# Retention attention and a Mish MLP on one core: half products of four feature blocks placed around the last outputs of the head, an earlier Mish table, factors in one operation

## The chip, the cores and the metric

The kernel runs on one core of a Trainium2 chip. The metric is the device time of one execution in microseconds; lower is better. A core has a matrix engine (TensorE, PE in the profile; its weight loads are PEld), a vector engine (VectorE, DVE), a scalar engine with function tables (ScalarE, ACT), a general engine (GpSimd, POOL) and a synchronisation engine (SyncE, SP). Each works through its own list of instructions in order and waits on semaphores. Products land in PSUM, which has eight banks of 512 float32 values in each of 128 partitions; everything else works out of SBUF. In this kernel POOL issues the loads and SP most stores.

## The reference, cut to what matters

```
# q, k, v: (8 batches, 8 heads, 576 positions, 64)
scores = q @ k.T / 8
gamma  = 1 - 2 ** (-5 - head)
Dmat   = where(i >= j, gamma ** (i - j), 0)
ret    = (scores * Dmat) @ v
x      = ret.transpose(0, 2, 1, 3).reshape(4608, 512)
h      = x @ w_in                      # 512 x 2048
g      = h * tanh(log(1 + exp(h)))     # Mish
out    = g @ w_out                     # 2048 x 512
```

## The kernel before

The 4608 tokens are cut into chunks of 128 (576 = 4 x 128 + 64, the last 64 of two batches make one chunk), and four chunks make a tile of 512 tokens. There are nine tiles. For each tile the attention gives xT (the features by the tokens, in four slices of 128 features), the first dense product with w_in gives 16 feature blocks f = 0 to 15 of 128, Mish on ScalarE turns each into gT, and the second dense product with w_out gives the output. The order of all instructions on each engine is written out by hand; from about 17 us on the dense products run on TensorE without a break, and the attention of later tiles is placed between them.

The change lies in the head, that is what runs before the dense products of the first tile. The first tile is the first 128 positions of batches 0 to 3, and no state is needed for it:

- Constants (L125 to L165). POOL's iota writes dist. VectorE makes late (L152), dist (L153), dmask for eight heads (L156), ident (L158) and pos (L160), then ex, one column of five per head (L661). ScalarE takes exponentials: dmask (L659), then gq (L662) and gv (L663).
- `f_transpose(t, g, i, parts)` turns k (i = 1) or q (i = 0) of the two batches of group g on TensorE (L203) into one or two PSUM banks, and each bank is evicted by the engine that parts names (L208).
- `f_scores(0, g)` makes the scores of two batches (L222), and VectorE multiplies them by dmask into sm (L226): four operations per group.
- `f_v(0, b, copy)` casts v of batch b into vb (L236).
- `f_out(0, b, copy)` is the product of vb and sm (L254), evicted into xT's columns of batch b (L258).
- `turn_back(g)` (L272) turns keys back for a later stage, and `keep_warm` (L170, L173) issues products of zeros.
- ScalarE's Mish table is loaded by a Mish of one column, warm (L674), between `f_v(0, 0)` and `f_v(0, 1)`.
- `g1_half(f)` (L565) multiplies only the first 256 columns of xT, the batches 0 and 1, for a feature block; `g1(0, f, 2, begun)` adds the other half and then runs Mish (L590). `g1_pair(2)` takes f = 2 and 3 whole, in two banks of two pools, with a Mish each at L577.
- `product` (L553) can be halved: two products of 256 columns (L558) take the place of one of 512. The count `halved` says how many of the next ones are.

PSUM is given out by pools: ps_sc has two tiles of two banks ("sc"), ps_st one bank ("st"), ps_h two of one bank ("hp"), ps_o one ("ops"). The framework sets the semaphores: an instruction waits for those before it in the program that touch the same data.

Of the kernel before, what the change touches and what calls it, by code (L numbers as in the profile page):

```python
# [9 lines left out]
F32 = mybir.dt.float32  # L10
BF16 = mybir.dt.bfloat16
AX = mybir.ActivationFunctionType
OP = mybir.AluOpType
# [3 lines left out]
def kernel(  # L17
# [18 lines left out]
    nc = tc.nc  # L36
    B, H, S, D = q.shape
    assert (B, H, S, D) == (8, 8, 576, 64)
    P = 128
# [4 lines left out]
    KC = d_model // P  # L44
    NCH = 4
# [17 lines left out]
    consts = ctx.enter_context(tc.tile_pool(name="consts", bufs=1))  # L63
# [7 lines left out]
    op = ctx.enter_context(tc.tile_pool(name="op", bufs=4))  # L71
    PS = bass.MemoryType.PSUM
    ps_sc = ctx.enter_context(tc.tile_pool(name="ps_sc", bufs=2, space=PS))
    ps_st = ctx.enter_context(tc.tile_pool(name="ps_st", bufs=1, space=PS))
    ps_h = ctx.enter_context(tc.tile_pool(name="ps_h", bufs=2, space=PS))
    ps_o = ctx.enter_context(tc.tile_pool(name="ps_o", bufs=1, space=PS))
# [4 lines left out]
    w_in_t = wpool.tile([P, KC, d_ff], BF16)  # L81
# [15 lines left out]
    gts = {0: gp.tile([P, nF, NCH * P], BF16, name="gT")}  # L97
# [29 lines left out]
    lnd = consts.tile([P, 1], F32)  # L127
# [5 lines left out]
    pos = consts.tile([P, 5], F32)  # L133
    for c in range(5):
        nc.vector.memset(pos[:, c:c + 1], float(P * c))
    nc.vector.memset(pos[64:P, 4:5], 512.0 - 64.0)
    minus_p = consts.tile([P, 1], F32)
    late = consts.tile([P, P], F32)
    for i in (1, 0):
        for b in (2, 3):  # L140
# [6 lines left out]
    for f0 in (512, 768):  # L147
        load_w_in(f0, 256)
    mask = consts.tile([P, 64], F32)
    lg = [math.log(1.0 - 2.0 ** (-5.0 - h)) for h in range(H)]  # L150
    nc.vector.tensor_copy(minus_p, dist[:, 0:1])
    nc.vector.tensor_scalar(late, dist, 0.0, 1.0e6, op0=OP.is_lt, op1=OP.mult)  # L152
    nc.vector.tensor_tensor(dist, dist, late, op=OP.max)  # L153
    dmask = consts.tile([P, H, P], F32)
    for h in range(H):
        nc.vector.tensor_scalar(dmask[:, h, :], dist, lg[h], None, op0=OP.mult)  # L156
    ex = consts.tile([P, 5, H], F32)
    nc.vector.tensor_scalar(ident, dist, 0.0, None, op0=OP.is_equal)  # L158

    nc.vector.tensor_scalar(pos, pos, minus_p, None, op0=OP.subtract)  # L160
    gqk = consts.tile([P, 5, 2, H], F32)
    nc.vector.memset(gqk, 1.0)
    gq = gqk[:, :, 0, :]
    gv = consts.tile([P, 5, H], F32)
    warm = consts.tile([P, 25], F32)  # L165

    def keep_warm(n, pool=ps_o, name="ops", long=0):
        idle = pool.tile([P, 512], F32, name=name)
# [6 lines left out]
    xts = {}  # L175
# [12 lines left out]
    def f_transpose(t, g, i, parts):  # L188

        name = ("qb", "kb")[i]  # L190
        out_t = tr.tile([P, 2, NP, P], BF16, name="qkT", bufs=6).rearrange("p i n t -> p (i n) t")
        n = 8 // len(parts)
        moves = []
        for j, (pool, tname, copy) in enumerate(parts):
            tp = pool.tile([P, 2, 8, P] if tname == "sc" else [P, 8, P], BF16, name=tname)
            tp = (tp[:, 0] if tname == "sc" else tp)[:, 0:n]
            for r in range(n):
                if t == 1:
                    mix = fst[1][name, "mix", g][:, n * j + r]
                    nc.tensor.transpose(tp[:, r, :], mix.rearrange("p x d -> p (x d)"), ident)  # L200
                else:
                    for x in range(2):
                        nc.tensor.transpose(tp[ds(64 * x, 64), r, :],  # L203
                                            fst[0][name][:, 2 * g + x, ts(n * j + r, D)], ident)
            moves.append((copy, out_t.rearrange("p h (g r) -> p h g r", r=8)[:, :, :, ds(n * j, n)],
                          tp.rearrange("p r (g h) -> p h g r", h=H)))
        for copy, to, src in moves:
            copy(to, src)  # L208
        fst[t][name, g] = out_t
# [21 lines left out]
    def f_v(t, b, copy):  # L231
        vb = first.tile([P, H, D], BF16, name="vb", bufs=4)
        copies = copy if isinstance(copy, tuple) else (copy,)
        n = H // len(copies)
        for j, copy in enumerate(copies):
            copy(vb[:, ds(n * j, n), :], v0[4 * t + b][:, ds(n * j, n), :])  # L236
        fst[t]["vb"][b] = vb
        if t == 1:
            v0s[4 + b] = vb

    def f_out(t, b, copy):
        if b == 0:
            xts[t] = xp.tile([P, KC, NCH * P], BF16, name="xT")
        vb = fst[t]["vb"][b]
        if t == 0:
            pool, name = ((ps_h, "hp"), (ps_h, "hp"), (ps_st, "st"), (ps_o, "ops"))[b]
            ot = pool.tile([P, NP, P], F32, name=name)
        else:
            if b % 2 == 0:
                fst[1]["out"] = ps_sc.tile([P, 2, NP, P], F32, name="sc")  # L250
            ot = fst[1]["out"][:, b % 2]
        for p in range(NP):
            for e in range(2):
                nc.tensor.matmul(ot[ds(64 * e, 64), p, :], lhsT=vb[:, 2 * p + e, :],  # L254
                                 rhs=fst[t]["sm", b][:, 2 * p + e, :],
                                 start=(p == 0), stop=True, skip_group_check=True)
        if t == 0:
            copy(xts[t][:, :, ts(b, P)], ot)  # L258
        elif b % 2:
            copy(xts[1].rearrange("p h (b i) -> p b h i", i=P)[:, ds(b - 1, 2)], fst[1]["out"])  # L260
# [285 lines left out]
    halved = [0]  # L546
# [4 lines left out]
    def product(to, w, x, first, last):  # L551
        if first or last or not halved[0]:
            newest[0] = nc.tensor.matmul(to, lhsT=w, rhs=x, start=first, stop=last)  # L553
            return
        halved[0] -= 1
        n = x.shape[-1] // 2
        for j in range(2):
            nc.tensor.matmul(to[:, ts(j, n)], lhsT=w, rhs=x[:, ts(j, n)], start=False, stop=False,  # L558
                             skip_group_check=True)

    def g1_half(f):
        hp = ps_h.tile([P, NCH * P], F32, name="hp")
        n = NCH * P // 2
        for c in range(KC):
            nc.tensor.matmul(hp[:, 0:n], lhsT=w_in_t[:, c, ts(f, P)], rhs=xts[0][:, c, 0:n],  # L565
                             start=(c == 0), stop=(c == KC - 1))
        return hp

    def g1_pair(f0):
        banks = [ps_o.tile([P, NCH * P], F32, name="ops"), ps_h.tile([P, NCH * P], F32, name="hp")]  # L570
        for cs in ((0, 1), (2, 3)):
            for f in range(2):
                for c in cs:
                    halved[0] = int(c == 1)
                    product(banks[f], w_in_t[:, c, ts(f0 + f, P)], xts[0][:, c, :], c == 0, c == KC - 1)
        for f in range(2):
            nc.scalar.activation(gts[0][:, f0 + f, :], banks[f], AX.Mish)  # L577

    def g1(t, f, parts=1, begun=None):
        if t not in gts:  # L580
            gts[t] = gp.tile([P, nF, NCH * P], BF16, name="gT")
        if begun is not None:
            hp = begun
        else:
            hp = ps_h.tile([P, NCH * P], F32, name="hp")
        n = NCH * P // parts
        for j in range(0 if begun is None else 1, parts):
            for c in range(KC):
                product(hp[:, ts(j, n)], w_in_t[:, c, ts(f, P)], xts[t][:, c, ts(j, n)], c == 0, c == KC - 1)
        done = nc.scalar.activation(gts[t][:, f, :], hp, AX.Mish)  # L590
        if (t, f) in gated:
            load(gated[t, f], done)
            queued[0] += 1
# [62 lines left out]
    dve, act, pool = nc.vector.tensor_copy, nc.scalar.copy, nc.gpsimd.tensor_copy  # L656


    nc.scalar.activation(dmask, dmask, AX.Exp, bias=lnd[:, 0:1])  # L659
    for h in range(H):  # L660
        nc.vector.tensor_scalar(ex[:, :, h], pos, lg[h], None, op0=OP.mult)  # L661
    nc.scalar.activation(gq, ex, AX.Exp)  # L662
    nc.scalar.activation(gv, ex, AX.Exp, scale=-1.0)  # L663
    for b in range(2):
        dve(fst[0]["qb"][:, b, :], q0[:, b, :])
    keep_warm(4, long=4)
    f_transpose(0, 0, 1, [(ps_h, "hp", act), (ps_h, "hp", dve)])
    f_transpose(0, 0, 0, [(ps_st, "st", act), (ps_o, "ops", dve)])
    keep_warm(1, ps_sc, "sc")
    f_transpose(0, 1, 1, [(ps_h, "hp", act), (ps_h, "hp", act)])  # L670
    f_scores(0, 0)
    f_transpose(0, 1, 0, [(ps_st, "st", act), (ps_o, "ops", act)])
    f_v(0, 0, pool)
    nc.scalar.activation(warm[:, 0:1], lnd, AX.Mish)  # L674
    f_v(0, 1, act)
    load_w_in(1024, 512)
    keep_warm(1, ps_h, "hp", long=1)
# [7 lines left out]
    load_w_in(1536, 512)  # L685
    f_v(0, 3, (dve, dve))
    f_v(0, 2, (act, pool))
    f_out(0, 3, dve)
    f_out(0, 2, act)
    begun = [g1_half(0), g1_half(1)]  # L690
    for i, b in ((1, 0), (1, 1), (0, 0), (0, 1)):
        load_first_qk(1, i, b)
    for i in range(2):
# [20 lines left out]

    for f in range(2):
        g1(0, f, 2, begun[f])
    g1_pair(2)
    for f in range(4, nF):
        halved[0] = (f > 6) + (f > 8)
        g1(0, f)  # L720
    for i in range(2):
        f_mix(0, i)
# [1 line left out]
    for i in range(nF):  # L724
        for step in steps.get(i, "").split():
            n = int(step[1])
# [171 lines left out]
```

## Time and profile before

| | us |
|---|---|
| median of 3 runs | 296.61 |
| lowest and highest | 296.42, 296.66 |
| the profiled execution | 297.28 |
| its span, first to last instruction | 295.6 |
| TensorE busy in the span | 286.1 |
| VectorE, ScalarE, POOL busy | 140.0, 128.1, 124.9 |
| HBM read and written, MB | 37.75, 9.44 |

The profile is one execution seen by the hardware. A row of the timeline has the start in us from the span's start, the busy time, the engine, the line of the kernel, the operation, what it writes and reads, the shape and the count; in brackets stands how long the engine was idle before it and what ended that. In a row that merges several instructions the busy time is their union. Products on TensorE are pipelined: one of 128x512 is shown with 0.38 us, but the next can start earlier, so lengths of stages are better read off the starts. A row of waits names the waiting engine and line, what it waited for, the total in us, the count and the longest. Landings are times from the issue of a transfer to its last byte.

### The profile page before, as it was taken

To read this page: it belongs to the slowest core of one execution; us is meant where nothing else is said; L and a number is where in the kernel's file an instruction comes from. 1 tells how busy PE (TensorE), PEld (TensorE's weight loads), DVE (VectorE), ACT (ScalarE), POOL (GpSimd) and SP (SyncE) were. 2 spreads that over 40 slices of the span, in tenths; PEclk is the share of its full clock that TensorE was granted. 3 is DMA by queue.
4 is the path that set the end of the run, shared out by engine and by line. 5 is a ranking of instruction groups with operands and counts; after the bars stand their busy time and mean duration, and the time that the engine had idled before them with its cause. 6 is when DMAs were issued, how large, how long until landed. Compare 5 with 4: busy or idle time off the path is not lost.

```text
span 295.6 us, 7898 instructions
## 1 busy us (share of the span) xinstructions
PE 286.1 (97%) x3447; PEld 159.7 (54%) x3486; DVE 140.0 (47%) x252; ACT 128.1 (43%) x210; POOL 124.9 (42%) x163
## 2 busy tenths in 40 slices
PE   7899999999999999999999999999999999999995
PEld 4666887556567454447645454545454544444443
DVE  5861549399954829454655454535453221000011
ACT  3856226776545534443443434343435333333200
POOL 8944678880167195855483636392020000000000
PEclk9999999999999999999999999999999999999999
DMA  7999999982498889799476837374222111011121
GB/s 154 234 204 204 205 328 337 336 237 85 109 270 190 168 229 254 232 145 330 116 204 164 260 90 237 108 229 115 68 71 71 38 38 65 9 35 49 59 71 71
DMA packets 44067, 47.45 MB, mean 161 GB/s; under 512 B 25984, under 2 KB 33152, under 8 KB 44032
## 3 DMA queue, kind: packets, MB, share of 16 engines
q0 software_dynamic: 15120, 31.20, 41.6%
q1 hardware_dynamic: 28768, 15.54, 20.7%
q8 instruction: 27, 0.44, 0.6%
q10 hardware_dynamic: 144, 0.20, 0.2%
q14 instruction: 8, 0.07, 0.1%
HBM read 37.75 MB, written 9.44 MB: 160 GB/s over the span
## 4 chain that ended last, share of the span: by engine, by line
PE 93%; DMA 2%; issue 1%; ACT 1%; POOL 1%; DVE 0%; POOLq 0%
PE hp L553 41%; PE ops L553 30%; PE hp L558 6%; PE ops L558 4%; DMA gT<-in_q_dram 2%; PE sc L373 1%; PE sc L428 1%; PE hp L504 1%; PE hp L487 1%; PE hp L634 1%; PE st L558 1%; POOL gT L107 1%; PE st L428 1%; PE sc L351 1%; PE sc L200 1%
## 5 line engine op out<-in xcount | busy, mean ns | idle before, releaser
L553 PE MATMUL hp<-xT,w_in_t 128*128 128x512 bf16 (+1 forms) x505 | 125.9, 376 | 0.9
L590 ACT ACTIVATE gT<-hp 128x512 bf16<-128x512 f32 x142 | 84.8, 598 | 95.3 <-PE hp L553 88.8
L553 PE MATMUL ops<-w_out_t,gT 128*128 128x512 bf16 x403 | 99.9, 379 | 2.0 <-issue 1.9
L553 PEld LDWEIGHTS <-w_in_t 128*128 128x128 bf16 x527 | 51.4, 98 | 53.9 <-issue 0.4
L553 PEld LDWEIGHTS <-gT 128*128 128x128 bf16 x470 | 44.7, 98 | 51.3
L642 DVE COPY res<-ops 128x512 f32<-128x512 f32 x28 | 19.3, 690 | 85.3 <-PE ops L553 85.2
L330 DVE TENSOR_TENSOR qks<-qkraw,gqk 128x512 bf16<-128x512 f32 x56 | 36.9, 709 | 0.0
L307 POOL DMA_DIRECT2D qkraw<-in_q_dram x24 | 21.5, 898 | 23.5 <-ACT gT L590 15.0
L337 POOL TENSOR_TENSOR vs<-vraw,gv 128x512 bf16<-128x512 f32 x16 | 16.8, 1068 | 25.0 <-PE hp L487 25.0
L516 DVE CAST xT<-hp 128x512 bf16<-128x512 f32 x13 | 9.0, 691 | 30.8 <-PE hp L504 30.8
L307 POOL DMA_DIRECT2D vraw<-in_v_dram x24 | 21.8, 907 | 1.8 <-DMA vraw<-in_v_dram 1.0
L307 POOL DMA_DIRECT2D qkraw<-in_k_dram x24 | 21.3, 886 | 1.0 <-DMA vpair<-in_v_dram 0.7
L516 ACT CAST xT<-hp 128x512 bf16<-128x512 f32 x14 | 8.2, 586 | 28.5 <-PE hp L504 28.5
L558 PEld LDWEIGHTS <-gT 128*128 128x128 bf16 x180 | 17.3, 98 | 3.7
L464 DVE TENSOR_TENSOR total<-sc,total 128x256 f32<-128x256 f32 x40 | 16.9, 422 | 1.0
L379 DVE TENSOR_TENSOR sm<-sc,mask 128x1024 bf16<-128x1024 f32 x14 | 17.0, 1214 | 0.6 <-PE sc L373 0.6
L558 PE MATMUL hp<-xT,w_in_t 128*128 128x256 bf16 x104 | 15.9, 272 | 0.0
L558 PEld LDWEIGHTS <-w_in_t 128*128 128x128 bf16 x106 | 10.4, 98 | 6.6 <-issue 0.2
L522 POOL COPY held<-qkT 128x1 bf16<-128x1 bf16 x8 | 1.5, 189 | 27.8 <-DMA qkT<-qks 27.8
L467 ACT CAST ssb<-total 128x768 bf16<-128x768 f32 (+3 forms) x13 | 11.6, 895 | 3.2 <-DVE total L464 3.2
L558 PE MATMUL ops<-w_out_t,gT 128*128 128x256 bf16 x96 | 12.4, 273 | 0.2
L553 PE MATMUL hp<-w_out_t,gT 128*128 128x512 bf16 x49 | 12.0, 379 | 0.2 <-issue 0.2
(132 smaller groups left out, 243.3 us busy)
## 6 DMA issues: line engine op xcount, KB each, us to landing
out_dram<-res SPq DMA_DIRECT2D x31, 256.0 KB, 2.4
qkraw<-in_q_dram POOLq DMA_DIRECT2D x24, 256.0 KB, 4.4
qkraw<-in_k_dram POOLq DMA_DIRECT2D x24, 256.0 KB, 4.5
vraw<-in_v_dram POOLq DMA_DIRECT2D x24, 256.0 KB, 4.7
w_out_t<-in_moe_w_out_dram POOLq DMA_DIRECT2D x4, 512.0 KB, 12.3
gT<-in_k_dram POOLq DMA_DIRECT2D x8, 128.0 KB, 7.1
gT<-in_v_dram POOLq DMA_DIRECT2D x2, 512.0 KB, 6.6
w_in_t<-in_moe_w_in_dram POOLq DMA_DIRECT2D x2, 512.0 KB, 10.3
```

What stands on the lines that cost most here:

```text
L307: ins = nc.gpsimd.dma_start(out=t, in_=src[b, :, ds(P * c, P), :].rearrange("h p d -> p h d"))
L330: nc.vector.tensor_tensor(slots[:, :, y], heads[:, :, y], factors[:, :, y].unsqueeze(3).to_broadcast([P, NP, 2, D]), op=OP.mult)
L337: engine.tensor_tensor(vs, live[n]["v"], gv[:, c, :].unsqueeze(2).to_broadcast([P, H, D]), op=OP.mult)
L379: nc.vector.tensor_tensor(sm.rearrange("p e x n i -> p (e x n) i"), live[n]["sc"].rearrange("p e x n i -> p (e x n) i"), mask.unsqueeze(1) ...
L428: ins = nc.tensor.matmul(to, lhsT=ks, rhs=vs, start=(x is not None or j == 0 and p == 0), stop=True, skip_group_check=True)
L464: nc.vector.tensor_tensor(new[:, k], st[:, j, x], total[b], op=OP.add)
L467: casts.append(lambda copy: copy(lows[:, 0:k], new[:, 0:k]))
L516: copy(xts[t][:, :, ds(P * s, 2 * P)].rearrange("p h (x j i) -> p j h x i", x=2, j=2)[:, j], both[j])
L553: newest[0] = nc.tensor.matmul(to, lhsT=w, rhs=x, start=first, stop=last)
L558: nc.tensor.matmul(to[:, ts(j, n)], lhsT=w, rhs=x[:, ts(j, n)], start=False, stop=False, skip_group_check=True)
L590: done = nc.scalar.activation(gts[t][:, f, :], hp, AX.Mish)
L642: copy(ot, ops)
```

## The change

It does four things.

1. The logarithms of the eight factors are put into a small constant lgs by eight memsets at the start, beside the memset of gqk. pos and ex are computed ahead of late, dist and dmask, and ex by one operation with broadcasts in place of eight.
2. ScalarE takes the exponentials gq and gv first, then that of dmask, and directly behind it the one-column Mish that loads the table, ahead of the first evictions.
3. In the first two `f_transpose` calls VectorE takes the first bank of each and ScalarE the second (the other way round before).
4. `g1_half(0)` and `g1_half(1)` move ahead of `f_out(0, 3)` and `f_out(0, 2)`. Behind these a new `g1_pair_half(2)` multiplies the first 256 columns for f = 2 and 3, into the two banks of one tile of ps_sc. After the second halves of f = 0 and 1, `g1` adds the second halves of f = 2 and 3 and runs their Mish. `g1_pair` goes. The halved products of the later blocks are set anew: one in each of f = 6 to 15, where it was one in f = 7 and 8 and two in f = 9 to 15. The number of TensorE's instructions stays the same.

warm gets smaller by as many columns as lgs has.

```diff
@@ constants
+    lg = [math.log(1.0 - 2.0 ** (-5.0 - h)) for h in range(H)]
+    gqk = consts.tile([P, 5, 2, H], F32)
+    nc.vector.memset(gqk, 1.0)
+    gq = gqk[:, :, 0, :]
+    lgs = consts.tile([P, H], F32)
+    for h in range(H):
+        nc.vector.memset(lgs[:, h:h + 1], lg[h])
...
     nc.vector.tensor_copy(minus_p, dist[:, 0:1])
+    nc.vector.tensor_scalar(pos, pos, minus_p, None, op0=OP.subtract)
+    ex = consts.tile([P, 5, H], F32)
+    nc.vector.tensor_tensor(ex, pos.unsqueeze(2).to_broadcast([P, 5, H]),
+                            lgs.unsqueeze(1).to_broadcast([P, 5, H]), op=OP.mult)
     nc.vector.tensor_scalar(late, dist, 0.0, 1.0e6, op0=OP.is_lt, op1=OP.mult)
...
-    nc.vector.tensor_scalar(pos, pos, minus_p, None, op0=OP.subtract)
-    gqk = consts.tile([P, 5, 2, H], F32)
-    nc.vector.memset(gqk, 1.0)
-    gq = gqk[:, :, 0, :]
     gv = consts.tile([P, 5, H], F32)
-    warm = consts.tile([P, 25], F32)
+    warm = consts.tile([P, 17], F32)
@@ first dense product
-    def g1_pair(f0):
-        banks = [ps_o.tile([P, NCH * P], F32, name="ops"), ps_h.tile([P, NCH * P], F32, name="hp")]
+    def g1_pair_half(f0):
+        banks = ps_sc.tile([P, 2, NCH * P], F32, name="sc")
+        n = NCH * P // 2
         for cs in ((0, 1), (2, 3)):
             for f in range(2):
                 for c in cs:
-                    halved[0] = int(c == 1)
-                    product(banks[f], w_in_t[:, c, ts(f0 + f, P)], xts[0][:, c, :], c == 0, c == KC - 1)
-        for f in range(2):
-            nc.scalar.activation(gts[0][:, f0 + f, :], banks[f], AX.Mish)
+                    nc.tensor.matmul(banks[:, f, 0:n], lhsT=w_in_t[:, c, ts(f0 + f, P)], rhs=xts[0][:, c, 0:n],
+                                     start=(c == 0), stop=(c == KC - 1))
+        return banks
@@ the head's order
-    nc.scalar.activation(dmask, dmask, AX.Exp, bias=lnd[:, 0:1])
-    for h in range(H):
-        nc.vector.tensor_scalar(ex[:, :, h], pos, lg[h], None, op0=OP.mult)
     nc.scalar.activation(gq, ex, AX.Exp)
     nc.scalar.activation(gv, ex, AX.Exp, scale=-1.0)
+    nc.scalar.activation(dmask, dmask, AX.Exp, bias=lnd[:, 0:1])
+    nc.scalar.activation(warm[:, 0:1], lnd, AX.Mish)
...
-    f_transpose(0, 0, 1, [(ps_h, "hp", act), (ps_h, "hp", dve)])
-    f_transpose(0, 0, 0, [(ps_st, "st", act), (ps_o, "ops", dve)])
+    f_transpose(0, 0, 1, [(ps_h, "hp", dve), (ps_h, "hp", act)])
+    f_transpose(0, 0, 0, [(ps_st, "st", dve), (ps_o, "ops", act)])
...
     f_v(0, 0, pool)
-    nc.scalar.activation(warm[:, 0:1], lnd, AX.Mish)
     f_v(0, 1, act)
...
+    begun = [g1_half(0), g1_half(1)]
     f_out(0, 3, dve)
     f_out(0, 2, act)
-    begun = [g1_half(0), g1_half(1)]
+    pair = g1_pair_half(2)
...
     for f in range(2):
         g1(0, f, 2, begun[f])
-    g1_pair(2)
+    for f in range(2):
+        g1(0, 2 + f, 2, pair[:, f])
     for f in range(4, nF):
-        halved[0] = (f > 6) + (f > 8)
+        halved[0] = int(f > 5)
         g1(0, f)
```

More of the change, by code (lines that the diff above doesn't have):

```diff
@@ L149 @@
     mask = consts.tile([P, 64], F32)
-    lg = [math.log(1.0 - 2.0 ** (-5.0 - h)) for h in range(H)]
     nc.vector.tensor_copy(minus_p, dist[:, 0:1])
+    nc.vector.tensor_scalar(pos, pos, minus_p, None, op0=OP.subtract)
+    ex = consts.tile([P, 5, H], F32)
+    nc.vector.tensor_tensor(ex, pos.unsqueeze(2).to_broadcast([P, 5, H]),
+                            lgs.unsqueeze(1).to_broadcast([P, 5, H]), op=OP.mult)
     nc.vector.tensor_scalar(late, dist, 0.0, 1.0e6, op0=OP.is_lt, op1=OP.mult)
@@ L156 @@
         nc.vector.tensor_scalar(dmask[:, h, :], dist, lg[h], None, op0=OP.mult)
-    ex = consts.tile([P, 5, H], F32)
     nc.vector.tensor_scalar(ident, dist, 0.0, None, op0=OP.is_equal)
-    nc.vector.tensor_scalar(pos, pos, minus_p, None, op0=OP.subtract)
-    gqk = consts.tile([P, 5, 2, H], F32)
-    nc.vector.memset(gqk, 1.0)
-    gq = gqk[:, :, 0, :]
     gv = consts.tile([P, 5, H], F32)
-    warm = consts.tile([P, 25], F32)
+    warm = consts.tile([P, 17], F32)
     def keep_warm(n, pool=ps_o, name="ops", long=0):
```

## The prediction

> **What bounds the kernel now.** I read the page first, then who waited for whom on TensorE from 17 us on, then the chain of waits, then the timelines of three engines up to 22 us, and last the landings of the weights. The run shown took 297.28 us in all, 1.68 us of it outside the span; the median of the runs is 296.61.
>
> ```profile
> span 295.6 us, 7898 instructions
> PE 286.1 (97%) x3447; PEld 159.7 (54%) x3486; DVE 140.0 (47%) x252; ACT 128.1 (43%) x210; POOL 124.9 (42%) x163
> ```
>
> TensorE sets the time. After the head it waits for no other engine and for no transfer, only for the hand-over between kinds of product:
>
> ```profile
> PE ops L553 <- issue: 1.9, 12, 0.2
> PE st L558 <- issue: 0.2, 1, 0.2
> PE hp L553 <- issue: 0.2, 1, 0.2
> ```
>
> So what moves TensorE's place at about 20 us moves the end by as much, as long as nothing else turns late. The change touches the first 30 us alone. There the chain of waits goes through q's transfer, two evictions of ScalarE and its table load (L674):
>
> ```profile
> 4.40 5.57 DMA gT<-in_q_dram
> ...
> 10.46 1.07 ACT qkT L208 x2
> ...
> 11.55 1.28 ACT L674
> ```
>
> TensorE's timeline (start, duration) shows what that costs:
>
> ```profile
> 12.74 0.41 PE L254 MATMUL hp<-sm,vb 128*64 128x128 bf16 x8
> 13.61 0.41 PE L254 MATMUL hp<-sm,vb 128*64 128x128 bf16 x8 [0.45 <-ACT vb L236]
> 13.95 1.07 PE L272 MATMUL sc<-ident,qkT 128*128 128x128 bf16 x16
> ...
> 15.38 0.41 PE L254 MATMUL ops<-sm,vb 128*64 128x128 bf16 x8
> 15.63 0.39 PE L254 MATMUL st<-sm,vb 128*64 128x128 bf16 x8
> 15.95 1.05 PE L565 MATMUL hp<-xT,w_in_t 128*128 128x256 bf16 x8
> 16.84 1.04 PE L553 MATMUL hp<-xT,w_in_t 128*128 128x256 bf16 x8
> 17.71 0.38 PE L553 MATMUL ops<-xT,w_in_t 128*128 128x512 bf16 x1
> ```
>
> Two outputs that nothing parts start 0.25 apart (15.38, 15.63). The second of the first pair could start at 12.74 + 0.25 = 12.99; it starts at 13.61, because its vb was cast behind the table load. The gap is worth 0.62 us. Behind 13.61 TensorE goes without a real stop, and I read lengths off the starts: output to turn-back 0.34, turn-back with its idle products 1.43, two outputs 0.57, eight half products 0.89, their second halves 0.87.
>
> ScalarE's timeline:
>
> ```profile
> 4.87 1.15 ACT L659 ACTIVATE dmask<-dmask,lnd 128x1024 f32<-128x1024 f32 x1 [2.78 <-DVE dmask L156]
> ...
> 7.46 0.59 ACT L208 COPY qkT<-hp 128x512 bf16<-128x512 bf16 x1 [0.88 <-PE hp L203]
> 7.94 0.59 ACT L208 COPY qkT<-st 128x512 bf16<-128x512 bf16 x1
> ...
> 10.94 0.59 ACT L208 COPY qkT<-ops 128x512 bf16<-128x512 bf16 x1
> ...
> 12.84 0.20 ACT L674 ACTIVATE warm<-lnd 128x1 f32<-128x1 f32 x1
> 12.95 0.60 ACT L236 CAST vb<-gT 128x512 bf16<-128x512 f32 x1
> 13.46 1.19 ACT L258 CAST xT<-hp 128x512 bf16<-128x512 f32 x2
> ...
> 16.06 0.59 ACT L258 CAST xT<-st 128x512 bf16<-128x512 f32 x1 [1.11 <-PE st L254]
> 17.47 1.09 ACT L590 ACTIVATE gT<-hp 128x512 bf16<-128x512 f32 x2 [0.82 <-PE hp L553]
> ```
>
> VectorE's timeline:
>
> ```profile
> 1.16 0.09 DVE L135 MEMSET pos<- 128x1 f32 x5
> 1.32 0.06 DVE L136 MEMSET pos<- 64x1 f32 x1
> 2.95 0.15 DVE L151 COPY minus_p<-dist 128x1 f32<-128x1 f32 x1 [1.57 <-POOL dist L130]
> 3.02 0.22 DVE L152 TENSOR_SCALAR late<-dist 128x128 f32<-128x128 f32 x1
> 3.27 0.29 DVE L153 TENSOR_TENSOR dist<-dist,late 128x128 f32<-128x128 f32 x1
> ...
> 4.89 0.22 DVE L160 TENSOR_SCALAR pos<-pos,minus_p 128x5 f32<-128x5 f32 x1
> ...
> 5.14 1.04 DVE L661 TENSOR_SCALAR ex<-pos 128x5 f32<-128x5 f32 x8
> ...
> 8.29 0.68 DVE L208 COPY qkT<-ops 128x512 bf16<-128x512 bf16 x1
> 9.55 4.95 DVE L226 TENSOR_TENSOR sm<-sc,dmask 128x512 bf16<-128x512 f32 x8 [0.58 <-ACT qkT L208]
> 14.42 0.48 DVE L236 CAST vb<-gT 128x256 bf16<-128x256 f32 x2
> 15.84 0.69 DVE L258 CAST xT<-ops 128x512 bf16<-128x512 f32 x1 [0.94 <-PE ops L254]
> ```
>
> **Factors in one operation, and their place.** Eight operations over 5 columns (1.04) become one over 40, and nine small memsets fall into VectorE's wait of 1.57 for the iota, where they cost nothing; without that cover nine at 0.03 (five start within 1.16 to 1.32) would cost 0.3. But pos and ex now stand ahead of late. pos takes 0.22. The one operation is not in the trace: it takes between 0.13 (1.04 / 8, five columns) and 0.29 (L153, 128 columns). With some overlap, late and the eight dmask rows behind it come 0.35 to 0.51 later; I take 0.45, as 40 columns lie between. The q casts come sooner, which nothing waits for.
>
> **Table sooner.** The exponential of dmask then starts at 4.87 + 0.45 = 5.32 and ends at 6.47. The load (1.28) with 0.02 ahead and the 0.11 from warm's start to the next copy let ScalarE copy from 7.88. It now takes the second key bank and ops: 7.88, then 0.48 later 8.36, end 8.95. The last copy of that group ended at 8.29 + 0.68 = 8.97 before. So VectorE's first sm stays at 9.55; by the bounds above, 0.1 sooner on ScalarE buys nothing and 0.06 later costs about 0.04. Behind the copy of 10.94 (end 11.53) vb is now cast at once and done at about 12.0, before TensorE asks at 12.99: the gap of 0.62 closes.
>
> The Trainium skill, ScalarE: Activation LUTs, section What ACT_TABLE_LOAD costs, has a switch at about 2.66 us, load and drain together. The rows here have load and warm at 11.55 to 12.95, 1.40 in all; by the page the copies would start at about 9.1 instead of 7.9.
>
> **Turn-back.** It needs the sixth of VectorE's eight products: 9.55 + 6 x 0.62 = 13.3. So it starts at 13.35 instead of 12.99 + 0.34 = 13.33; against 13.95 that is 0.60 gained.
>
> **Half products around the last outputs.** TensorE: 13.35 + 1.43 = 14.78 for f = 0, 1 (first two batches), 15.67 for the last outputs, 16.24 for the new halves of f = 2, 3, 17.13 for the second halves of f = 0, 1, 18.00 for f = 2, 18.44 for f = 3. No column of products is added: halves replace whole products, and the fewer halvings later (f > 5) give back the instructions. xT of the first two batches: the first output is evicted from 13.2 and the second from 13.7, so done at 14.3, ahead of 14.78; the last two, 0.46 and 0.43 behind their outputs, are done at 16.8 and 16.9, ahead of 17.13. vb of the outputs is ready at 14.9. The weights:
>
> ```profile
> L87 POOL DMA_DIRECT2D w_in_t<-in_moe_w_in_dram x1: 777/777/777, 7.5 to 7.5; - x1
> ...
> DMA to landing us min/median/max: 6.8/6.8/6.8
> ```
>
> ```profile
> L87 POOL DMA_DIRECT2D w_in_t<-in_moe_w_in_dram x1: 750/750/750, 9.0 to 9.0; - x1
> ...
> DMA to landing us min/median/max: 6.7/6.7/6.7
> ```
>
> The first lands at 14.3 (wanted 14.78), the third at 15.7 (wanted 16.7). Without anything else f = 4 would start at 18.87. Before, it started at 17.71 + 2 x 0.87 = 19.45.
>
> **The wait that is added.** f = 2 and 3 now share one tile of two banks of the pool sc, where the pair before had two tiles of two pools. In the order of the changed kernel's instructions the first second-half product of f = 3 carries a wait for ScalarE that f = 2 has not (L558 there is L553 here):
>
> ```
> 365 L558 Matmult sc<-xT,w_in_t 128x256
> 366 L558 Ldweights w_in_t
> 367 L558 Matmult sc<-xT,w_in_t 128x256 [waits Activation_49]
> ```
>
> The count it waits for is that of the Mish of f = 2, the reader of the tile's other bank. That Mish is third in a row on ScalarE. The first follows its products' start by 0.63 (16.84 to 17.47): 17.13 + 0.63 = 17.76. Two in a row take 1.09, one 0.59, so they start 0.50 apart: 18.26 and 18.76, and the third ends at 19.35. TensorE follows an eviction by 0.06 (12.95 + 0.60 to 13.61). f = 3 starts at 19.41 instead of 18.44: 0.97 lost. Behind it on TensorE wait all products from f = 4 on; f = 4 starts at 19.41 + 0.44 = 19.85, 0.40 later than before. Mish of f = 3 and 4 come later with it, so ScalarE adds no second wait, and the weights and q, k, w_out, being transfers of fixed times, are only more punctual.
>
> The Trainium skill, PSUM — Partial Sum Buffer, section PSUM bank collisions raise a hardware error, asks that engines be kept apart by bank and quadrant; f = 3 lies in another bank than the Mish reads. By that rule the wait could be absent, and f = 4 would start at 18.87; no run here shows it yet.
>
> **Sum.** -0.62 for the gap, +0.02 for the turn-back, +0.03 for rounding of hand-overs, +0.97 for the wait: +0.40 us. 297.28 becomes 297.68 in such a run; for the median, 296.61 + 0.40 = 297.0.
>
> **Rivals.**
> No stall: the tile's wait is over when TensorE comes to it, as when ScalarE's three Mish run earlier than I place them or the wait falls on one of f = 0 or 1. For it: the two banks are disjoint. Against it: the wait stands in the order, and three evictions of 0.50 spacing can't end before 18.44 when the first can't start before 17.76. It gives 18.87 against 19.45, -0.57: 296.0. It is the side on which the change pays.
>
> Slower by over the bound: the table load in its new place holds the first evictions. Its place is ScalarE between 6.4 and 7.9, and it decides from the point at which the ops copy ends behind 8.97; each 0.1 behind delays scores, sm, turn-back and all else by 0.1. For it: the margin is 0.02 and the operation that sets dmask back is not in the trace. Against it: even 0.29 for ex costs 0.04. With 0.2 to 0.3 on top of the stall: 297.2 to 297.4. By the 2.66 of the Trainium skill (ScalarE: Activation LUTs, What ACT_TABLE_LOAD costs) an estimate gives 298.2; the trace's 1.40 does not agree with it.
>
> The weights of f = 2, 3 come late: only if they land 0.5 later than in the run shown; 297.0 plus a few tenths, hidden in part by the same stall.
>
> **How the numbers follow.** The forecast has 0.62 (own range 296.75 to 297.35), no stall 0.13, the slower case with the late weights 0.25. Time 297.0. A measurement of this kernel can tell about 0.2% from no change, 0.59 us: 296.02 to 297.20. No stall lies at the lower bound: 0.09 of its 0.13 faster. Of the forecast a quarter, 0.16, lies above the upper one; of the slower case 0.22. Faster 0.09, same 0.53, slower 0.38. The range 296.5 to 297.6 leaves out no stall and what lies above 297.6 of the slower case, 0.2 together.
>
> **What would show it.** Right: no idle time ahead of the second output near 13.0; turn-back near 13.35; vb cast at about 11.4; half products at 14.8 and 16.2; a wait of TensorE for the Mish of about 0.8 to 1.0 near 18.4 to 19.4; f = 4 at about 19.85; all later starts some 0.4 later. Wrong: no idle time at 18.4 (then 296.0), sm later than 9.65, waits for w_in at 16.2, or a new wait behind 30 us.

## The result, and the profile after

The changed kernel takes 297.57 us (median of 6 runs, 297.55 to 297.86) where the kernel before, timed beside it, takes 296.51 (296.09 to 296.89). The ratio is 1.0039, with a 95% interval of 1.0026 to 1.0052: the change costs about 1.1 us. Run once more later, it gave 297.85 (297.56 to 298.06, 5 runs), ratio 1.0043 (1.0031 to 1.0056). Forecast were 297.0 and, as the likeliest case, a difference too small to tell; that the change would clearly cost time was given a chance of 0.38. The time lies inside the range that was given, 296.5 to 297.6, but only by 0.03, and the second median lies outside it, so that this end was met is luck.

The profile after was taken on an execution of 297.58 us:

```profile
span 295.9 us, 7938 instructions
```

Its TensorE timeline, against the rows of before in the prediction (TensorE's lines are 5 higher now: L227 the scores, L259 the output, L277 the turn-back, L570 the half products of f = 0 and 1, L558 the second halves and the whole products; L580, the half products of f = 2 and 3, is new):

```profile
9.06 0.62 PE L227 MATMUL sc<-qkT 64*128 64x128 bf16 x16
...
12.76 0.64 PE L259 MATMUL hp<-sm,vb 128*64 128x128 bf16 x16
13.33 1.07 PE L277 MATMUL sc<-ident,qkT 128*128 128x128 bf16 x16
...
14.67 1.04 PE L570 MATMUL hp<-xT,w_in_t 128*128 128x256 bf16 x8
15.63 0.41 PE L259 MATMUL ops<-sm,vb 128*64 128x128 bf16 x8
...
16.20 1.05 PE L580 MATMUL sc<-xT,w_in_t 128*128 128x256 bf16 x8
17.09 1.04 PE L558 MATMUL hp<-xT,w_in_t 128*128 128x256 bf16 x8
17.96 0.60 PE L558 MATMUL sc<-xT,w_in_t 128*128 128x256 bf16 x4
19.35 0.60 PE L558 MATMUL sc<-xT,w_in_t 128*128 128x256 bf16 x4 [0.79 <-ACT gT L595]
19.78 0.38 PE L558 MATMUL hp<-xT,w_in_t 128*128 128x512 bf16 x1
```

The two first outputs are now one row of 16 products with nothing between them, so the gap of 0.62 is closed. At 19.35 stands the wait that was forecast: the second half of f = 3 waits for the Mish of f = 2. From 17 us to the end this is the only wait of TensorE for another engine:

```profile
PE sc L558 <- ACT gT L595: 0.8, 1, 0.8
```

From the start of f = 4 to the end of the span it is 276.1 us in the changed kernel (19.78 to 295.9) as in the kernel before (19.45 to 295.6), so what the change costs lies ahead of f = 4, and the new places of the halved products cost nothing behind it.

ScalarE's timeline after shows both ends of the wait, the table load in its new place and the three Mish in a row:

```profile
6.55 1.28 ACT L667 ACT_TABLE_LOAD   x1
...
7.95 0.57 ACT L213 COPY qkT<-hp 128x512 bf16<-128x512 bf16 x1
8.42 0.59 ACT L213 COPY qkT<-ops 128x512 bf16<-128x512 bf16 x1
...
11.03 0.63 ACT L241 CAST vb<-gT 128x512 bf16<-128x512 f32 x1
...
17.73 1.08 ACT L595 ACTIVATE gT<-hp 128x512 bf16<-128x512 f32 x2 [0.83 <-PE hp L558]
18.70 0.60 ACT L595 ACTIVATE gT<-sc 128x512 bf16<-128x512 f32 x1
```

VectorE's first sm starts where it was forecast (9.55):

```profile
9.57 4.87 DVE L231 TENSOR_TENSOR sm<-sc,dmask 128x512 bf16<-128x512 f32 x8 [0.94 <-ACT qkT L213]
```

TensorE's starts from the turn-back on, and the last two rows of ScalarE, lie within 0.11 us of their forecast. The two profiled executions, of before and after, differ by 297.58 - 297.28 = 0.30, near the +0.40 of the sum. What failed is the step from that pair of executions to the median: the medians differ by 297.57 - 296.51 = 1.06. So the first question was whether the profile of before showed a usual execution.

### The profile page after: what moved, and what is told of

It is laid out like the page before. It is cut to its first block, busy times and chain, and to the rows that moved or that the text cites. A ratio compares the mean times of both kernels' runs of the same rounds, so it can differ in the third digit from the quotient of the medians.

```text
span 295.9 us, 7938 instructions
## 1 busy us (share of the span) xinstructions
PE 289.8 (98%) x3486; PEld 159.7 (54%) x3486; DVE 140.3 (47%) x253; ACT 127.8 (43%) x210; POOL 124.8 (42%) x163
## 4 chain that ended last, share of the span: by engine, by line
PE 94%; ACT 2%; DVE 2%; issue 1%; POOL 1%; POOLq 0%; DVEq 0%
PE hp L558 42%; PE ops L558 31%; PE hp L563 5%; PE ops L563 4%; PE sc L378 1%; PE sc L433 1%; PE hp L509 1%; PE hp L492 1%; PE hp L639 1%; PE st L563 1%; PE st L433 1%; DVE sm L231 1%; PE sc L356 1%; PE sc L227 1%; PE sc L205 1%
## 5 line engine op out<-in xcount | busy, mean ns | idle before, releaser
L558 PE MATMUL hp<-xT,w_in_t 128*128 128x512 bf16 (+1 forms) x527 | 128.8, 376 | 0.0
L558 PE MATMUL ops<-w_out_t,gT 128*128 128x512 bf16 x416 | 102.6, 379 | 0.0
L558 PEld LDWEIGHTS <-w_in_t 128*128 128x128 bf16 x535 | 52.1, 98 | 54.8 <-issue 1.2
L558 PEld LDWEIGHTS <-gT 128*128 128x128 bf16 x470 | 44.7, 98 | 51.3
L563 PE MATMUL hp<-xT,w_in_t 128*128 128x256 bf16 x90 | 14.4, 273 | 0.0
L558 PE MATMUL hp<-w_out_t,gT 128*128 128x512 bf16 x52 | 12.7, 379 | 0.0
L563 PEld LDWEIGHTS <-w_in_t 128*128 128x128 bf16 x90 | 8.8, 98 | 6.5 <-issue 0.2
```

## The experiments

Two theories stand behind the first experiments. L: the profiled execution of before was one in which k and q landed late; usually its head is faster and its gap small, while the changed kernel's evictions wait for the table load in any case. G: the gap of 0.6 is there in every run, and the rest of the cost comes from the half products.

**The kernel before, once more.**

> The kernel before, unchanged, for a second profile. Theory L (landings): the profile of before that the prediction read was an execution with late transfers; in the usual one the keys land near 6.3 and the queries near 9.2, as in the profile of the changed kernel, TensorE's second output starts near 13.1 instead of 13.61, f = 4 starts at 18.7 to 19.0 instead of 19.44 and the span is 295.0 or less. Theory G (gap): the head looks as in the first profile (gap of 0.45 ahead of the second output, f = 4 at 19.4, span 295.6), and the 0.66 that the change costs over the predicted 0.40 lies behind 20 us or outside the span. Ratio 1.000 by both.

296.61 (296.21 to 297.02, 12 runs), ratio 0.9999 (0.9988 to 1.0010). The profile is of an execution of 296.44 with a span of 294.7, some 0.85 shorter than in the profile of the prediction. Its TensorE, ScalarE and VectorE timelines:

```profile
8.62 0.62 PE L222 MATMUL sc<-qkT 64*128 64x128 bf16 x16
...
12.33 0.86 PE L254 MATMUL hp<-sm,vb 128*64 128x128 bf16 x16
13.12 1.07 PE L272 MATMUL sc<-ident,qkT 128*128 128x128 bf16 x16
...
15.12 1.05 PE L565 MATMUL hp<-xT,w_in_t 128*128 128x256 bf16 x8
```

```profile
10.72 1.28 ACT L674 ACT_TABLE_LOAD   x1
...
12.12 0.60 ACT L236 CAST vb<-gT 128x512 bf16<-128x512 f32 x1
```

```profile
9.13 4.88 DVE L226 TENSOR_TENSOR sm<-sc,dmask 128x512 bf16<-128x512 f32 x8 [0.57 <-ACT qkT L208]
```

In the profile of the prediction TensorE had waited for k and for q, and the chain of waits went through q's transfer:

```profile
7.01 0.63 PE L203 MATMUL hp<-ident,gT 128*64 128x128 bf16 x15 [0.41 <-DMA gT<-in_k_dram]
...
10.01 0.41 PE L203 MATMUL st<-ident,gT 128*64 128x128 bf16 x7 [0.18 <-DMA gT<-in_q_dram]
```

The repeat has neither wait: the q loads of batches 2 and 3 landed 4.4 us after their issue (median) instead of 5.5, and its chain goes back to TensorE's products of zeros, which end at 6.64. So the loads are not of fixed times, as the prediction took them.

The table load starts at 10.72 instead of 11.55, because q was evicted sooner; the cast of vb is done at 12.72, and the second output starts some 0.2 late instead of 0.62 (from the first output to the turn-back it is 0.79 here, 0.57 in the changed kernel). From the turn-back on everything stands 0.83 earlier than in the profile of the prediction (13.12 against 13.95), half of it (8.62 against 9.04) already at the scores, half from the smaller gap. f = 4 starts at 18.61, a little sooner even than L said. Against this execution the changed kernel's turn-back, at 13.33, is 0.21 later, not 0.60 sooner. L holds for this execution; that it is the usual one is seen from the times: of 30 more runs of the kernel before, timed beside this one, four took 297.28 or longer, and their median is 296.53.

**The table part alone**: the kernel before with parts 1 to 3 of the change, part 4 left out (the constants, edited as in the change, are not shown).

```diff
...
-    nc.scalar.activation(dmask, dmask, AX.Exp, bias=lnd[:, 0:1])
-    for h in range(H):
-        nc.vector.tensor_scalar(ex[:, :, h], pos, lg[h], None, op0=OP.mult)
     nc.scalar.activation(gq, ex, AX.Exp)
     nc.scalar.activation(gv, ex, AX.Exp, scale=-1.0)
+    nc.scalar.activation(dmask, dmask, AX.Exp, bias=lnd[:, 0:1])
+    nc.scalar.activation(warm[:, 0:1], lnd, AX.Mish)
...
-    f_transpose(0, 0, 1, [(ps_h, "hp", act), (ps_h, "hp", dve)])
-    f_transpose(0, 0, 0, [(ps_st, "st", act), (ps_o, "ops", dve)])
+    f_transpose(0, 0, 1, [(ps_h, "hp", dve), (ps_h, "hp", act)])
+    f_transpose(0, 0, 0, [(ps_st, "st", dve), (ps_o, "ops", act)])
...
     f_v(0, 0, pool)
-    nc.scalar.activation(warm[:, 0:1], lnd, AX.Mish)
     f_v(0, 1, act)
```

> The kernel before with the factors, the earlier table and the swapped evictions of the change, but g1_pair and the order of half products as before. Theory L: nothing gained: 296.5 to 296.8, ratio 1.000 to 1.001. Theory G: the gap goes, and the last outputs wait 0.1 to 0.2 for vb: 295.9 to 296.1, ratio 0.998.

296.67, ratio 1.0001 (0.9991 to 1.0011): the part that was to bring 0.62 brings nothing in the median. Its 12 runs lie between 296.66 and 296.78, while the 30 runs of the kernel before spread from 296.11 to 297.40. The early load takes the early runs away together with the late ones.

**The changed kernel, once more.**

> The changed kernel, unaltered, once more. Theory L: its head is set by the table load and by the stall at f = 3, not by how early q and k land, so its runs lie close together, 297.55 to 297.9, and no run of it falls under 297.5, while the kernel before spreads over a microsecond. If the wait for w_in seen in the version with no stall is common in it too, some runs reach 298.0 to 298.3.

297.85 (297.56 to 298.06, 5 runs). In its profiled execution (297.56) the last k load landed at 7.99, in that of the first run at 7.67, and the last q at 9.42 and 9.18, yet the scores start at 9.06 and f = 4 at 19.78 in both, to the hundredth. The chain of waits through its head in the first profiled run says why (start, length, what):

```profile
5.38 1.15 ACT dmask L666
...
6.55 1.28 ACT L667
...
7.84 0.20 ACT warm L667
8.05 0.97 ACT qkT L213 x2
...
9.06 0.41 PE sc L227 x8
```

In front of it stand VectorE's constants, and no transfer. The ops copy (8.42 + 0.59) ends at 9.01 in both, though k and q landed 0.2 to 0.3 apart. No run of eleven falls under 297.5, and five lie between 297.55 and 297.58; but six stand above 297.6, two of them at 298.01 and 298.06, so something varies in this kernel too. The next two experiments show a candidate.

**No stall**: the changed kernel with the second halves of f = 2 and 3 ahead of both Mish.

```diff
     for f in range(2):
-        g1(0, 2 + f, 2, pair[:, f])
+        for c in range(KC):
+            product(pair[:, f, NCH * P // 2:], w_in_t[:, c, ts(2 + f, P)], xts[0][:, c, NCH * P // 2:],
+                    c == 0, c == KC - 1)
+    for f in range(2):
+        nc.scalar.activation(gts[0][:, 2 + f, :], pair[:, f], AX.Mish)
```

> The changed kernel with the second halves of f = 2 and 3 both issued ahead of the two Mish, so that f = 3 waits for no Mish. Both theories: f = 4 starts 0.9 sooner than in the changed kernel (18.9 instead of 19.78). Theory L: about 296.6 to 296.8, ratio 1.000 to 1.001 to before, as the rest of the change gains nothing against a usual execution of before. Theory G, the prediction's sum without its wait: 0.57 below before, 296.0, ratio 0.998.

297.02 (296.70 to 297.46, 12 runs), ratio 1.0011 (1.0000 to 1.0021): 0.55 less than the changed kernel's first median (0.83 less than its second), not the 0.9 expected, and between what L and G said. TensorE's timeline:

```profile
15.01 1.05 PE L570 MATMUL hp<-xT,w_in_t 128*128 128x256 bf16 x8 [0.18 <-DMA w_in_t<-in_moe_w_in_dram]
...
18.31 1.04 PE L558 MATMUL sc<-xT,w_in_t 128*128 128x256 bf16 x8
19.19 1.03 PE L558 MATMUL hp<-xT,w_in_t 128*128 128x512 bf16 x4
```

The stall is gone (f = 2 and 3 are one row of eight), but the moved half products start at 15.01 instead of 14.67, behind w_in, which the kernel before asked for only at 15.12. Its issue (durations in ns) and landing in this run:

```profile
L87 POOL DMA_DIRECT2D w_in_t<-in_moe_w_in_dram x1: 780/780/780, 7.7 to 7.7; - x1
...
DMA to landing us min/median/max: 7.2/7.2/7.2
```

It landed at 14.96 here, at 14.27 and 13.8 in the two profiles of the changed kernel, which have no such wait.

**The load back**: the changed kernel with the one-column Mish between the two casts of vb, as before.

```diff
-    nc.scalar.activation(warm[:, 0:1], lnd, AX.Mish)
...
     f_v(0, 0, pool)
+    nc.scalar.activation(warm[:, 0:1], lnd, AX.Mish)
     f_v(0, 1, act)
```

> The changed kernel with the one-column Mish, and so the table load, back between the first two casts of v; all else as changed. Theory L: ScalarE's first eviction starts near 7.1 again instead of 7.95 and the first sm near 9.2 instead of 9.57; the second output waits for vb again until 13.1 or 13.2; the stall of f = 3 stays: 297.4 to 297.8, within 0.2 of the changed kernel. Theory G: the gap of 0.6 is back: 298.1 to 298.2.

297.82 (297.64 to 298.20, 7 runs), ratio 1.0037 (1.0023 to 1.0052): no gain, just above what L said. The profile is of an execution of 298.12, one of the two slowest of the seven. In it the head does get faster (turn-back 13.06 instead of 13.33), and the wait for w_in takes that and more:

```profile
8.40 0.62 PE L227 MATMUL sc<-qkT 64*128 64x128 bf16 x16
...
12.43 0.70 PE L259 MATMUL hp<-sm,vb 128*64 128x128 bf16 x16 [0.25 <-POOL vb L241]
13.06 1.07 PE L277 MATMUL sc<-ident,qkT 128*128 128x128 bf16 x16
...
15.22 1.05 PE L570 MATMUL hp<-xT,w_in_t 128*128 128x256 bf16 x8 [0.67 <-DMA w_in_t<-in_moe_w_in_dram]
```

So the next question was what is left of the cost in the version with no stall. W: it is the wait for w_in alone, which part 4 brings because it asks for w_in sooner (at 14.67, where the table part alone has 15.36).

**The half products back behind the outputs**, in the version with no stall:

```diff
-    begun = [g1_half(0), g1_half(1)]
     f_out(0, 3, dve)
     f_out(0, 2, act)
+    begun = [g1_half(0), g1_half(1)]
```

> The changed kernel with the second halves of f = 2 and 3 ahead of both Mish (no stall), and the half products of f = 0 and 1 back behind the last outputs. Theory W (behind the stall, what is left of the cost is the wait of those half products for the first w_in slice, now asked for 0.6 us sooner): as the kernel before with the early table alone, 296.6 to 296.8. Rival R (cutting f = 2 and 3 into halves costs by itself): stays at the 297.0 of the version with no stall.

296.74 (eight of 11 runs between 296.73 and 296.75; 297.49 the highest), ratio 1.0011 (1.0002 to 1.0020). W holds and R falls: cutting f = 2 and 3 into halves costs next to nothing (296.74 against the 296.67 of the table part alone; the kernel before, timed beside each group of these experiments, had medians of 296.53, 296.57 and 296.55). The profile caught the highest run, in which the halves of f = 3 waited 0.59 for a later slice of w_in.

**w_in earlier**: the version with no stall, half products ahead of the outputs, and its first w_in load ahead of the second v load.

```diff
     load_first_v(0)
-    load_first_v(2)
     load_w_in(0, 256)
+    load_first_v(2)
```

> The changed kernel with no stall (second halves of f = 2 and 3 ahead of both Mish), its half products of f = 0 and 1 still ahead of the last outputs, and the first w_in load issued ahead of the v load of batches 2 and 3. Theory W (what is left of the cost in the version with no stall, 297.02, is the wait of these half products for w_in): no wait for w_in near 14.7, turn-back still near 13.3, 296.6 to 296.8. Rival V (the later v takes its place: the last outputs wait for vb): 296.9 to 297.4. Rival R (the place itself costs, whatever lands): 297.0.

296.73 (ten of 11 runs between 296.70 and 296.75), ratio 1.0008 (1.0000 to 1.0017). W holds again; V and R fall. TensorE's timeline:

```profile
14.67 1.04 PE L570 MATMUL hp<-xT,w_in_t 128*128 128x256 bf16 x8
...
17.96 1.04 PE L558 MATMUL sc<-xT,w_in_t 128*128 128x256 bf16 x8
18.84 1.46 PE L558 MATMUL hp<-xT,w_in_t 128*128 128x512 bf16 x5
```

This version is the cleanest measure of the stall. It starts the half products at 14.67 and f = 2 at 17.96, as the changed kernel does, and f = 4 at 18.84 instead of 19.78: the stall costs 0.94 there, and 0.84 between the profiled executions (296.72, and 297.56 in the second profile of the changed kernel).

**q made late, in both kernels**: a quarter of the first w_in load is issued ahead of the q loads of batches 2 and 3.

```diff
     for i in (1, 0):
+        if i == 0:
+            load_w_in(0, 256, ts(0, 1))
         for b in (2, 3):
             load_first_qk(0, i, b)
...
-    load_w_in(0, 256)
+    load_w_in(0, 256, ds(1, 3))
```

> The kernel before, with a quarter of the first w_in load issued by GpSimd ahead of the two q loads of batches 2 and 3, so that q lands some 0.6 us later. Theory L (how early these loads land sets the head of the kernel before; the profiled run of before was one with late landings): the second group's scores, the first outputs and f = 4 come some 0.4 to 0.6 later; 296.9 to 297.2 against 296.53. Rival G (what the gap costs is there in every run and landings do not matter): 296.4 to 296.6.

> The changed kernel with the same q loads made late. Theory L: its first evictions wait for the table load and its second scores for VectorE's sm, so 0.6 us of lateness of q is hidden: 297.5 to 297.7 against 297.57 for the changed kernel, its f = 4 still near 19.8. Rival G, or a head bound by transfers in both kernels: as much later as the kernel before with late q, 298.0 or more.

The kernel before goes to 297.34 (296.87 to 298.29, 10 runs), ratio 1.0029 (1.0018 to 1.0041), more than L said. The changed one gives 297.67 (297.63 to 298.03, 5 runs), within its own runs. So one moves and the other does not, as L says. But the run of before does not show that q's landing did it. TensorE's and VectorE's timelines:

```profile
8.26 0.41 PE L205 MATMUL st<-ident,gT 128*64 128x128 bf16 x7 [0.66 <-DVE gT L667]
...
9.72 0.62 PE L224 MATMUL sc<-qkT 64*128 64x128 bf16 x16
```

```profile
5.76 2.45 DVE L667 CAST gT<-gT 128x512 bf16<-128x512 f32 x2
```

The two casts of q of batches 0 and 1 took 2.45 where the repeat of before has 1.19, and the first scores, which do not use the late q at all, came at 9.72 instead of 8.62. From there to the first output it is 3.70, as in the repeat (8.62 to 12.33). The run shows that lateness in this head goes straight to the end in the kernel before (297.54 - 296.44 = 1.10 for 1.10 at the scores); what made it late was another thing than meant. Nor is the pair a fair one: in the run of the changed kernel the same two casts took 0.75, so it never met that lateness. L rests on the repeat, and on the narrow spread of times with the early load, not on this pair.

**The load one place later**: the kernel before with the one-column Mish behind both casts of vb.

```diff
     f_v(0, 0, pool)
-    nc.scalar.activation(warm[:, 0:1], lnd, AX.Mish)
     f_v(0, 1, act)
+    nc.scalar.activation(warm[:, 0:1], lnd, AX.Mish)
```

> The kernel before with the one-column Mish, and so the table load, moved one place later on ScalarE: behind the cast of batch 1's vb, where ScalarE has nothing to do until the first output. Theory L: what the gap costs in a usual run is 0.2, in a late one 0.6, and here it goes without holding the evictions: 296.1 to 296.4. Rival S (VectorE's sm sets the turn-back in any case): 296.4 to 296.6. Rival T (the load now holds the evictions of the first outputs and so the half products): 296.6 to 296.9.

> The kernel before with only the table load moved behind the cast of batch 1's vb, once more: 296.1 to 296.4, 0.2 to 0.4 under the kernel before.

296.21 (11 runs), ratio 0.9990 (0.9980 to 1.0000), and the second time 296.37 (11 runs), ratio 0.9993 (0.9984 to 1.0003). ScalarE and TensorE in the first:

```profile
10.40 0.62 ACT L236 CAST vb<-gT 128x512 bf16<-128x512 f32 x1
11.04 1.28 ACT L675 ACT_TABLE_LOAD   x1
...
12.48 1.07 ACT L258 CAST xT<-hp 128x512 bf16<-128x512 f32 x2
```

```profile
12.02 0.64 PE L254 MATMUL hp<-sm,vb 128*64 128x128 bf16 x16
12.59 1.07 PE L272 MATMUL sc<-ident,qkT 128*128 128x128 bf16 x16
```

This profile is of one of the two fastest of the 11 runs (296.07). The load now lies where ScalarE has nothing to do, 11.04 to 12.32, between the cast and the first output's eviction. The gap is gone (0.57 from output to turn-back), and the load stands behind the evictions of k and q, as in the kernel before. In the second profile (296.37) v landed later, the load started at 11.63, and it held the first output's eviction to 13.03, some 0.5 us; TensorE did not wait for it, and the gap is gone there too.

**The same with the changed kernel's factors and swapped evictions**, f = 2 and 3 as before the change.

> The changed kernel's first part alone (factors in one operation, the first evictions swapped), with the table load behind the cast of batch 1's vb and f = 2 and 3 as before the change. If the factors and the swap shorten the head: 295.9 to 296.1. If the head is bound by transfers, as the kernel before with only the load moved seems to show (w_in landed at 14.56, its first product started at 14.62): 296.1 to 296.4.

296.28 (296.08 to 296.58, 11 runs), ratio 0.9990 (0.9981 to 0.9999), beside 296.37 for the simpler edit. The factors and the swap add nothing that these runs can tell. That this head is bound by transfers is not confirmed: w_in's first slice landed at 14.36, and its first product started at 14.95 without a wait. The medians of both versions lie under both kernels, by 0.18 to 0.36 us against before; the three intervals end at 0.9999, 1.0000 and 1.0003, so a gain over before is likely and not quite shown.

## Why the prediction was wrong

Point by point, in the order of its steps:

- **Factors in one operation**: right. The exponential of dmask starts at 5.38 (forecast 5.32).
- **Table sooner, its effect on the evictions**: this is the step that failed. "So VectorE's first sm stays at 9.55" was true only beside the one execution of before that was profiled, in which k and q landed late: there the scores started at 9.04 and sm at 9.55, in the repeat at 8.62 and 9.13. The changed kernel's sm came where it was forecast, at 9.57, but the early load puts a floor under the head (ops copy done at 9.01, scores at 9.06) which the repeat of before undercuts by 0.44 (its ops copy ended at 8.56).
- **The gap, -0.62**: the term was mis-sized for the median. "The gap is worth 0.62 us" is right for the execution shown; in the repeat it is about 0.2. With the floor against it, the table part alone measured +0.14 (296.67 against 296.53), with an interval that includes no change, where the prediction's terms gave -0.60.
- **Turn-back**: forecast 13.35, came at 13.33.
- **Half products around the last outputs**: forecast 14.78, 15.67, 16.24, 17.13, 18.00, came at 14.67, 15.63, 16.20, 17.09, 17.96. That w_in is ready in time ("lands at 14.3, wanted 14.78") held in both profiles of the changed kernel, with 0.4 or more to spare. In the profiles of two of its variants it lands at 14.96 and 15.18, and the wait (0.2 and 0.7) is not hidden by the stall, since the Mish behind it are pushed back as well: in the version with the load back, which has the stall, the half products start 0.55 later than in the changed kernel and f = 4 starts 0.57 later (20.35).
- **The wait that is added, +0.97**: right, 0.94 by the starts. The Mish of f = 2 was forecast to end at 19.35 and ended at 18.70 + 0.60 = 19.30.
- **The sum, "for the median, 296.61 + 0.40"**: here the fault became a number. The 0.67 between the profiled execution of before and its median was taken as an offset that both kernels share. It was the lateness of that execution, and it was the same lateness that made the gap look large. In the medians it is +0.14 for the table part and about 0.9 for the stall: 1.0 to 1.1, as measured. What lifts some runs of the changed kernel to 298 stays open; the wait for w_in is the candidate, but neither of its two profiles has it.

Of the rivals, "slower by over the bound: the table load in its new place holds the first evictions" names the mechanism that decided, with the right point (ops copy behind where it ended before). Its price of 0.2 to 0.3 was too low (the floor costs 0.44 against the repeat), and perhaps its chance, because 8.97 was taken as the usual end of that copy. "The weights of f = 2, 3 come late" was right in kind for the variants: f = 0 and 1 waited for w_in in two of their profiles, f = 3 in one. "No stall" did not occur: f = 3 waited 0.79 for the Mish that reads the other bank of its tile.

The Trainium skill, ScalarE: Activation LUTs, section What ACT_TABLE_LOAD costs, has 2.66 us for a switch, of which about 1.28 are the load. The load agrees with the trace (1.28); a drain behind it does not show here: from the load's start at 6.55 to the next copy at 7.95 it is 1.40.

## What to carry to other kernels

Before a term is read off a profile, the profiled execution's time is set beside the median: where it lies clearly above (297.28 and 296.61 here), an idle time in it may be a lateness that the other runs don't have, and then it is not there to be gained. A fixed piece of work put ahead of a stage whose start varies from run to run sets a floor under that stage, also in the runs in which it could start early; the better place was one line further, between the cast and the first eviction, where nothing waited for it in either profile. Two accumulators in one PSUM tile were one thing to the framework's semaphores here: all the products that fill them go ahead of the first read, as in the version with no stall. The other way out is a tile each: f = 0 and 1, which have that, take the same order of second halves and Mish, and their eight products run without a wait (17.09).

## What was not expected of the hardware

GpSimd's issue of the first v load, the same instruction each time, took 1.21 us in some profiles, 1.67 or 2.01 in others, with w_in's issue behind it starting at 7.52, 7.73 or 8.07 and its landing at 13.8 to 14.4, 14.8 to 15.2 or 15.2 (in the versions with the change's factors and the whole of w_in behind both v loads). It goes with VectorE's operations beside it. The changed kernel:

```profile
4.91 1.21 POOL L118 DMA_DIRECT2D gT<-in_v_dram  x1
```

```profile
5.27 0.90 DVE L167 TENSOR_SCALAR ident<-dist 128x128 bf16<-128x128 f32 x1
5.41 1.36 DVE L669 CAST gT<-gT 128x512 bf16<-128x512 f32 x2
```

The version with w_in earlier:

```profile
4.92 2.01 POOL L118 DMA_DIRECT2D gT<-in_v_dram  x1
```

```profile
5.27 0.22 DVE L167 TENSOR_SCALAR ident<-dist 128x128 bf16<-128x128 f32 x1
5.41 0.75 DVE L669 CAST gT<-gT 128x512 bf16<-128x512 f32 x2
```

In these two GpSimd is quick where VectorE's ident and casts are slow, and the other way round; where the issue took 1.67, as in the version with no stall, ident took 0.22 and the casts 1.40. Whether the order goes with the version or with the execution these runs do not tell: the changed kernel's two profiles agree, and most versions have only one. The Trainium skill, SBUF — State Buffer, section SBUF: two separate sides, describes a port pair that the two engines share as an exclusive lock, which blocks the writing of descriptors. The rows agree with that, but no run took one of the two away, so the cause is argued and not shown, and so is any part of it in why some runs of the changed kernel are slower than others.
